# Second pass in chunks of up to 32 tiles spread in three pieces, in place of 24 tiles in two

## The chip, the cores and the metric

The kernel runs on one NeuronCore of a Trainium2 chip. The metric is device time in microseconds (us) of one launch; lower is better. Engines are named as the profile names them: PE (TensorE, the matmuls), PEld (its weight loads), DVE (VectorE), ACT (ScalarE), POOL (GpSimd), SP (the queue that issues most plain DMAs).

## What is computed

A graph layer over N = 10,000 nodes and E = 640,000 edges, all in float32. Each edge takes the row of its source node (64 channels by 4 components, 1 KB), multiplies it by an edge weight and a small coupling tensor, and adds the result into its destination node.

```python
R = silu(edge_feat @ w_rad)                      # (E, 64)
xs = x[src]                                      # (E, 64, 4)
tp = einsum('eci,ef,ifo->eco', xs, Y, cg)        # (E, 64, 4)
msg = R[:, :, None] * tp
agg = segment_sum(msg.reshape(-1, 256), dst, N).reshape(N, 64, 4)
return einsum('ncm,cd->ndm', agg, w_mix)
```

## The kernel before

**Sorting edges by destination.** A sum over edges can only be a matmul when the edges of one tile share a small range of destinations. So the edges are sorted twice. An edge travels as 9 float32 numbers (`W = 9`: a packed key of source and destination, 4 of `Y`, 4 of `edge_feat`), 36 bytes. The first pass (`pass1`) reads edges in tiles of 128 and routes them into 20 groups of nodes in DRAM (`grp`). The second pass (`pass2`) reads one group and routes it into 16 buckets of up to 32 nodes each (`bkt`). The edges come in three parts of 30, 35.5 and 34.5 %, so that the message stage of one part runs while later parts are still being sorted.

**One routing step** (`route`, both passes). A chunk is a run of up to `T` tiles, here 24 in both passes. Per chunk:

- `places` (PE, lines 585 and 586) and `placed` (DVE, 596) and `slots` (DVE, 605 to 607) turn counts into a row and a slot for every edge.
- The chunk is handled in pieces; before, two halves. Per piece, `spread` (DVE, 617 and 623) writes each edge's 9 numbers into its slot of a wide row `X`, and `onehots` writes a 128 by 128 matrix `oh` for each tile that says which row an edge goes to. Of a piece's tiles ACT makes the last `self.act` (6 in the second stage of the program; lines 639 and 640), DVE the others (635).
- `move` (PE, 650) does one matmul per tile, `oh` as weights and `X` as the moving operand, into one PSUM bank `pr` of the chunk. A tile can only fall into slots `lo[t]` to `hi[t]`, so its matmul is `9 * (hi[t] - lo[t])` columns wide: 36 for the first tile of a chunk, 144 for the 24th of the second pass.
- `evict` (ACT, 660, and 662 for the rest of the row) copies the bank to SBUF as `rt`, and `store` (POOL, 669) writes it with one indirect DMA: 128 rows of `S` slots of 36 bytes, S = 35 in the second pass.

The step of a piece is `k`; `evict`, `move`, `places` and the rest run at fixed distances from it (`lag`, `ls` and the constants 5 to 8 in `route`).

**Messages** (`messages`). A unit is one bucket's tiles of one part, 5 or 6 tiles. POOL gathers the source rows, one indirect DMA per tile (944); PE turns and multiplies the edge features (987, 999); ACT applies silu (1003); DVE multiplies (1014, 1021); PE sums 12 matmuls per unit (1032); the sum goes to `Gp` or `Gs` (1061, 1063); at the end `mix` (1080) applies `w_mix`. Gathers run 5 units ahead, into 7 buffers `xg`.

**What sets the order.** In the second stage PE, DVE and ACT keep the order in which the code emits the work; `groups` emits the messages' quarter steps and, between them, as many steps of pass 1 of the next part and of pass 2 of the next group as each needs to be done in time (`pass2_steps` counts them). POOL and SP take their DMAs in a row each. Tables of a group (`tables`) are made once for one or two groups, with one row per chunk.

**After the last unit**, `overflow` handles edges that found no place, 640 at a time, in a loop whose count is read on the chip.

The lines on which the change bears most:

```python
def pieces(self, m):

    return [(0, (m + 1) // 2), ((m + 1) // 2, m)]
...
self.p2 = Pass(T, MB, P // MB, rates, 1.5, 5e-9)
...
v = max(m - self.act, 0)
```

## Time and profile before

| | |
|---|---|
| time, median of 3 runs | 8055.66 us (8052.32 to 8060.37) |
| span of the profiled execution | 9825.7 us |
| mean granted PE clock in it | 0.826 |
| busy share of its span: PE, DVE, ACT, POOL | 74 %, 66 %, 40 %, 59 % |
| indirect DMAs on POOL: gathers, stores of pass 1, stores of pass 2 | 5321, 240, 260 |

The profiled execution is longer than the timed runs; the page has no other time of it than its span. The program has three stages in that span: pass 1 of the first part alone (to 570 us), the mixed stage (pass 1 of the other parts until about 6300 us, pass 2 until about 9450 us, messages until 9740 us), and the overflow at the end. A row of a group of instructions reads: line, engine, operation, out<-in, shapes, count | busy us, mean ns of one | idle us of the engine ahead of them, and what ended it. "issue" is idle time that the profile explains by nothing; "remote" is a wait whose releaser it can't name. On POOL the time between the starts of two DMAs says more than the busy share, as DMA-issuing time is partly not counted. One matmul in float32 leaves two records of MATMUL, so x24 are 12 matmuls.

### The profile page before, as it was taken

The numbers are of one execution on the slowest core, as the hardware profiler recorded it, in microseconds if no ns is written. First come the engines' busy times: TensorE is split into PE (matmuls) and PEld (weight loads), VectorE is DVE, ScalarE is ACT, GpSimd is POOL, SyncE is SP. The second block draws the span as 40 slices with busy tenths as digits, with TensorE's granted clock in tenths as the row PEclk, the third lists the DMA queues.
The fourth block names the chain that finished last, engine by engine and source line by source line (L and its number), as shares of the span: only waits on it lengthen the run. The fifth ranks groups of instructions, "written<-read, shape, count | busy, mean of one in ns | idle before, by whom it ended". The sixth has DMA issues, their size and how long they took to land. (4 is left out here: it accounts for less than half of the span.)

```text
span 9825.7 us, 140823 instructions
## 1 busy us (share of the span) xinstructions
PE 7295.1 (74%) x49703; PEld 6709.1 (68%) x49703; DVE 6455.1 (66%) x10943; ACT 3911.8 (40%) x10964; POOL 5796.5 (59%) x6162
## 2 busy tenths in 40 slices
PE   7968877777776777777777777666776777776765
PEld 6867777777776776766767776666676666666664
DVE  8966777767765766777777776565555565555543
ACT  5754544445543443433434344232232332332321
POOL 4645555555556655555565655666666666666664
PEclk8978888888888888888888888787787888878787
DMA  4323333333333334444444443444433434334332
GB/s 185 109 71 105 105 102 101 99 105 102 107 97 113 109 103 116 114 118 116 115 116 113 123 115 111 127 120 121 113 111 111 115 109 115 111 109 111 103 111 67
DMA packets 680536, 1086.77 MB, mean 111 GB/s; under 512 B 255617, under 2 KB 485099, under 8 KB 673552
## 3 DMA queue, kind: packets, MB, share of 16 engines
q0 software_dynamic: 282224, 774.70, 27.8%
q1 hardware_dynamic: 397600, 303.00, 10.4%
q8 instruction: 395, 6.47, 0.3%
q14 instruction: 317, 2.60, 0.1%
HBM read 855.30 MB, written 222.83 MB: 110 GB/s over the span
## 5 line engine op out<-in xcount | busy, mean ns | idle before, releaser
L944 POOL DMA_INDIRECT xg<-in_x_dram,sidx x5321 | 5067.0, 952 | 3304.7 <-issue 1405.5
L1032 PE MATMUL G<-S,xg 128*128 128x128 f32 x21284 | 3317.3, 320 | 961.2 <-issue 391.9
L1032 PEld LDWEIGHTS G<-S,xg 128*128 128x128 f32 x21284 | 3099.7, 231 | 1070.4 <-issue 481.2
L650 PE MATMUL pr<-X,oh 128*128 128x117 f32 (+15 forms) x20530 | 3037.3, 306 | 694.6 <-issue 424.8
L650 PEld LDWEIGHTS pr<-X,oh 128*128 128x128 f32 x20530 | 2837.2, 214 | 858.9 <-issue 515.0
L1021 DVE TENSOR_TENSOR xg<-xg,pre 128x1536 f32<-128x1536 f32 (+1 forms) x939 | 1556.7, 1658 | 293.2 <-ACT pre L1003 158.9
L639 ACT ACTIVATE oh<-i,row 128x128 f32<-128x128 f32 x5322 | 1653.7, 391 | 81.7 <-remote 29.1
L1003 ACT ACTIVATE pre<-pre 128x384 f32<-128x384 f32 (+1 forms) x939 | 429.9, 458 | 3137.0 <-remote 1191.7
L623 DVE TENSOR_TENSOR X<-dv,Wt 128x1512 f32<-128x1512 f32 (+12 forms) x814 | 1337.0, 1642 | 345.2 <-remote 149.6
L1014 DVE TENSOR_TENSOR S<-dv,pay 128x768 f32<-128x768 f32 (+1 forms) x939 | 857.6, 913 | 140.1 <-remote 70.4
L640 ACT ACTIVATE oh<-oh,ones 128x768 f32<-128x768 f32 (+1 forms) x1000 | 862.8, 863 | 32.2
L1061 DVE TENSOR_TENSOR Gs<-old,G 128x256 f32<-128x256 f32 x313 | 131.6, 421 | 1063.2 <-remote 635.9
L635 DVE TENSOR_TENSOR oh<-dv,row 128x768 f32<-128x768 f32 (+3 forms) x960 | 796.0, 834 | 0.1
L991 ACT ACTIVATE sT<-pre 108x256 bf16<-108x256 bf16 x939 | 353.8, 377 | 800.0 <-remote 475.4
L596 DVE TENSOR_REDUCE pos<-pp 128x24 f32<-128x480 f32 (+9 forms) x500 | 267.4, 535 | 528.5 <-remote 333.3
L987 PE MATMUL pre<-idb,E 128*108 128x128 bf16 x1878 | 297.2, 243 | 341.9 <-DVE xg L1021 130.2
L987 PEld LDWEIGHTS <-E 128*108 128x108 bf16 x1878 | 234.1, 145 | 417.9 <-issue 213.4
L999 PE MATMUL pre<-wr,sT 108*128 108x192 bf16 x1878 | 334.3, 261 | 223.1 <-ACT sT L991 137.7
L669 POOL DMA_INDIRECT bkt<-rt,idx x260 | 259.5, 998 | 312.7 <-ACT rt L662 146.8
L1061 DVE TENSOR_TENSOR Gp<-old,G 128x256 f32<-128x256 f32 x313 | 130.8, 418 | 476.8 <-remote 324.5
L999 PEld LDWEIGHTS <-sT 108*128 108x128 bf16 x1878 | 185.6, 108 | 306.8 <-ACT sT L991 155.3
L669 POOL DMA_INDIRECT grp<-rt,idx x240 | 276.7, 1153 | 174.0 <-issue 51.3
(304 smaller groups left out, 4598.7 us busy)
## 6 DMA issues: line engine op xcount, KB each, us to landing
xg<-in_x_dram,sidx POOLq DMA_INDIRECT x5321
sums<-Gp SPq DMA_DIRECT2D x626, 128.0 KB
old<-sums SPq DMA_DIRECT2D x626, 128.0 KB
bkt<-z SPq DMA_DIRECT2D x26, 1024.0 KB
grp<-z SPq DMA_DIRECT2D x23, 1024.0 KB
pay<-bkt SPq DMA_DIRECT2D x208, 54.0 KB
out_dram<-ot SPq DMA_DIRECT2D x69, 128.0 KB
ys<-in_Y_dram SPq DMA_DIRECT2D x65, 96.0 KB
```

Source lines behind the costliest of these rows:

```text
L623: eng.tensor_tensor(X[:, b:e], msk[:, b:e].unsqueeze(3).to_broadcast([P, e - b, w, W]), CH[c][1][:, a + b:a + e, :].unsqueeze(2).to_broadc ...
L635: nc.vector.tensor_tensor(oh[:, :v, :], self.v128.unsqueeze(1).to_broadcast([P, v, P]), row[:, a:a + v].unsqueeze(2).to_broadcast([P, v, P ...
L639: nc.scalar.activation(oh[:, u], self.i128[:, :oh.shape[2]], AF.Square, bias=row[:, a + u:a + u + 1], scale=-1.0)
L640: nc.scalar.activation(oh[:, v:m], oh[:, v:m], AF.Relu, bias=self.ones[:, 0:1], scale=-2.0)
L650: nc.tensor.matmul(PR[c][:, ps.lo[t] * W:ps.hi[t] * W], oh[:, u, :], Xs[u], start=(t == 0), stop=(t == sizes[c] - 1), skip_group_check=True)
L669: nc.gpsimd.indirect_dma_start(out=ps.dst, out_offset=bass.IndirectOffsetOnAxis(ap=idx[:Q, i:i + 1], axis=0), in_=RT.pop(c), in_offset=None)
L944: nc.gpsimd.indirect_dma_start(out=xg[:, t, :], out_offset=None, in_=self.x, in_offset=bass.IndirectOffsetOnAxis(ap=si[:, u:u + 1], axis=0))
L987: nc.tensor.transpose(to[:108, h * P:(h + 1) * P], E[:, o + h * 108:o + h * 108 + 108], self.idb)
L999: nc.tensor.matmul(R[:, h * 192:h * 192 + n * 64], sT[:n * 36, h * P:(h + 1) * P], self.wr[:n * 36, :n * 64], start=True, stop=True)
L1014: nc.vector.tensor_tensor(S[:, :ut], self.eq[:, :ut].unsqueeze(3).to_broadcast([P, ut, NB, 4]), pb[:, :, 1:5].unsqueeze(2).to_broadcast([P ...
L1021: nc.vector.tensor_tensor(V, V, R.unsqueeze(3).to_broadcast([P, ut, 64, 4]), op=OP.mult)
L1032: nc.tensor.matmul(G[:, h].rearrange("p n f -> p (n f)"), V[:, t, 32 * h:32 * h + 32, :].rearrange("p c i -> p (c i)"), S[:, t].rearrange( ...
```

## The change

`Pass` gets a number of pieces, `cuts`: 2 for the two kinds of pass 1, as before, and 3 for the second pass, whose `T` goes from 24 to 32. A piece has at most `H = ceil(T / cuts)` tiles, so 11 in place of 12, and `pieces` cuts a chunk evenly into as few pieces as fit. Pass 1's chunks come out as before.

With these numbers and the same tiles (5265 in pass 2), the code's own planning gives:

| second pass | before | after |
|---|---|---|
| chunks, each with one store | 260 (160 in the first two parts, 100 in the last) | 200 (120 and 80) |
| pieces | 520 (480 of 9 to 12 tiles, 40 of 3) | 560 (540 of 8 to 11 tiles, 20 of 6) |
| slots S, bytes of a stored row | 35, 1260 | 45, 1620 |
| matmul columns, mean per tile; largest | 100; 144 | 112.8; 171 |
| tiles wider than 144 columns | 0 | 645 (450 in the first two parts) |
| numbers written into `X`, per partition | 638,766 | 687,339 |
| `oh` made by DVE, by ACT (tiles) | 2265, 3000 | 1905, 3360 |

`route` finds the steps of a chunk by its first piece (`first`) in place of by even and odd `k`; the distances in pieces stay. `rt` of pass 2 has 2 buffers in place of 3. `oh` is 12 tiles in both passes.

```diff
-    def __init__(self, T, B, R, rates, low, miss):
-        self.T, self.B, self.R, self.Q, self.H = T, B, R, B * R, (T + 1) // 2
+    def __init__(self, T, B, R, rates, low, miss, cuts=2):
+        self.T, self.B, self.R, self.Q, self.cuts, self.H = T, B, R, B * R, cuts, -(-T // cuts)
...
     def pieces(self, m):
 
-        return [(0, (m + 1) // 2), ((m + 1) // 2, m)]
+        at = [0] + list(itertools.accumulate(even(m, self.H)))
+        return list(zip(at, at[1:]))
...
-        N, E, T = self.N, self.E, 24
+        N, E, T, T2 = self.N, self.E, 24, 32
...
-        self.p2 = Pass(T, MB, P // MB, rates, 1.5, 5e-9)
+        self.p2 = Pass(T2, MB, P // MB, rates, 1.5, 5e-9, cuts=3)
...
+        self.H = max(late.H, self.p2.H)
...
+        first = {k: c for k, (c, a, _) in enumerate(pieces) if a == 0}
...
-            oh = self.ph.tile([P, ps.H, P], F, name="oh", bufs=3)
+            oh = self.ph.tile([P, self.H, P], F, name="oh", bufs=3)
...
-            rt = RT[c] = self.ph.tile([P, ps.S * W], F, name="rt", tag="rt" + ps.key, bufs=self.rt_bufs)[:Q, :n]
+            rt = RT[c] = self.ph.tile([P, ps.S * W], F, name="rt", tag="rt" + ps.key, bufs=2 if ps.cuts > 2 else self.rt_bufs)[:Q, :n]
...
-            if k % 2 and 0 <= k + 7 < NP:
+            if k + 7 in first:
...
-                places((k + 7) // 2)
-            if k % 2 == 0 and 0 <= k + 6 < NP:
-                placed((k + 6) // 2)
+                places(first[k + 7])
+            if k + 6 in first:
+                placed(first[k + 6])
...
-            if k % 2 and 0 <= k + 5 < NP:
-                slots((k + 5) // 2)
+            if k + 5 in first:
+                slots(first[k + 5])
...
-        n = 2 * len(self.sizes2(k, g))
+        n = sum(len(self.p2.pieces(m)) for m in self.sizes2(k, g))
```

Where instructions stand differently, at two places. First POOL, in the last part, over the stores of one group; `xg` are gathers (x6: six, one unit), `bkt` the stores of pass 2. Before:

```order
L669 DMA bkt_64<-rt_59179,idx_57043 1951488x9
L944 DMA xg_59314<-in_x_dram,sidx_58377 128x256 x6
L944 DMA xg_59400<-in_x_dram,sidx_58377 128x256 x6
L669 DMA bkt_64<-rt_59282,idx_57043 1951488x9
L944 DMA xg_59471<-in_x_dram,sidx_58377 128x256 x6
L669 DMA bkt_64<-rt_59372,idx_57043 1951488x9
L944 DMA xg_59534<-in_x_dram,sidx_58377 128x256 x6
L669 DMA bkt_64<-rt_59510,idx_57043 1951488x9
L944 DMA xg_59574<-in_x_dram,sidx_59390 128x256 x6
L944 DMA xg_59610<-in_x_dram,sidx_59390 128x256 x6
L669 DMA bkt_64<-rt_59572,idx_57043 1951488x9
```

And now:

```order
L672 DMA bkt_64<-rt_60122,idx_58984 1964288x9
L947 DMA xg_60301<-in_x_dram,sidx_59370 128x256 x6
L947 DMA xg_60371<-in_x_dram,sidx_59370 128x256 x6
L672 DMA bkt_64<-rt_60274,idx_58984 1964288x9
L947 DMA xg_60443<-in_x_dram,sidx_59370 128x256 x6
L947 DMA xg_60490<-in_x_dram,sidx_60291 128x256 x6
L672 DMA bkt_64<-rt_60469,idx_58984 1964288x9
L947 DMA xg_60526<-in_x_dram,sidx_60291 128x256 x6
L672 DMA bkt_64<-rt_60488,idx_58984 1964288x9
```

A group of the last part has four stores where it had five, and one or two units of gathers stand between two of them; the row of gathers itself is the same.

Second PE, in the last part, over the `move` matmuls of one chunk: `pr` is the chunk's bank, the second number of the shape the width. Before, a whole chunk of 21 tiles in its two pieces:

```order
L650 MATMUL pr<-X,oh 128x36
L650 MATMUL pr<-X,oh 128x54 x2
L650 MATMUL pr<-X,oh 128x72
L650 MATMUL pr<-X,oh 128x81 x3
L650 MATMUL pr<-X,oh 128x90 x2
L650 MATMUL pr<-X,oh 128x99
L650 MATMUL pr<-X,oh 128x108 x3
L650 MATMUL pr<-X,oh 128x117 x3
L650 MATMUL pr<-X,oh 128x135 x4
L650 MATMUL pr<-X,oh 128x144 x2
```

And now, the third piece of a chunk, behind a unit's sum (`G`), and the first piece of the next chunk:

```order
L1035 MATMUL G<-S,xg 128x128 x12
L653 MATMUL pr<-X,oh 128x144 x5
L653 MATMUL pr<-X,oh 128x162 x4
L653 MATMUL pr<-X,oh 128x36
L653 MATMUL pr<-X,oh 128x54 x2
L653 MATMUL pr<-X,oh 128x72
L653 MATMUL pr<-X,oh 128x81 x3
L653 MATMUL pr<-X,oh 128x90 x2
L653 MATMUL pr<-X,oh 128x99
```

The bank of a chunk is now filled by a third run of wider matmuls before the narrow ones of the next chunk begin.

## Rows read from the trace of the kernel before

**Rows 1.** The page's first block: busy us (share of the span), instructions.
```profile
PE 7295.1 (74%) x49703; PEld 6709.1 (68%) x49703; DVE 6455.1 (66%) x10943; ACT 3911.8 (40%) x10964; POOL 5796.5 (59%) x6162
```

**Rows 2.** Busy time by stage: stretch, length, engines (instructions), PE clock, DMA, GB/s.
```profile
0.00:570.00 570.00, 478.29 (x3426) 420.09 (x3427) 506.71 (x1257) 374.81 (x1161) 302.03 (x416) 0.89 0.37 132
570.00:800.00 230.00, 163.82 (x1090) 147.09 (x1090) 152.84 (x314) 111.96 (x318) 113.33 (x117) 0.78 0.32 89
800.00:6300.00 5500.00, 4199.30 (x29102) 3876.92 (x29102) 3876.03 (x6207) 2432.67 (x6784) 3200.78 (x3337) 0.84 0.39 110
6300.00:9450.00 3150.00, 2251.92 (x14880) 2084.32 (x14880) 1774.21 (x2881) 946.29 (x2572) 1993.17 (x2097) 0.81 0.40 113
9450.00:9700.00 250.00, 149.45 (x907) 136.70 (x907) 97.42 (x132) 33.20 (x89) 162.90 (x173) 0.78 0.39 111
9700.00:9826.00 126.00, 52.38 (x305) 44.03 (x305) 47.85 (x154) 12.90 (x42) 24.27 (x26) 0.69 0.10 27
```

**Rows 3.** Timeline of PE from 7599 us: start, us, instruction, [idle before].
```profile
7601.19 0.23 PE L650 MATMUL pr<-X,oh 128*128 128x81 f32 x1 [1.89 <-issue]
7602.59 0.29 PE L650 MATMUL pr<-X,oh 128*128 128x81 f32 x1 [1.17 <-issue]
```

**Rows 4.** Timeline of POOL from 7604 us.
```profile
7604.40 0.94 POOL L944 DMA_INDIRECT xg<-in_x_dram,sidx  x1 [2.67 <-remote]
7605.65 0.95 POOL L944 DMA_INDIRECT xg<-in_x_dram,sidx  x1 [0.30 <-issue]
...
7620.71 1.00 POOL L669 DMA_INDIRECT bkt<-rt,idx  x1 [0.30 <-issue]
```

**Rows 5.** Groups by line on POOL, 800 to 6300 us.
```profile
L944 POOL DMA_INDIRECT xg<-in_x_dram,sidx x3051 | 2911.5, 954 | 2106.0 <-issue 797.0 <-PE G L1032 622.3 <-remote 250.4
L669 POOL DMA_INDIRECT grp<-rt,idx x145 | 148.9, 1027 | 75.9 <-issue 39.5 <-ACT rt L660 21.0 <-DVE X L623 7.7
L669 POOL DMA_INDIRECT bkt<-rt,idx x141 | 140.9, 999 | 117.6 <-issue 35.1 <-ACT rt L660 25.0 <-ACT rt L662 18.5
```

**Rows 6.** Groups by line on POOL, 6300 to 9450 us.
```profile
L944 POOL DMA_INDIRECT xg<-in_x_dram,sidx x1991 | 1888.8, 949 | 1030.9 <-issue 529.5 <-remote 288.9 <-PE G L1032 99.9
L669 POOL DMA_INDIRECT bkt<-rt,idx x106 | 105.9, 999 | 126.2 <-ACT rt L662 70.1 <-issue 23.0 <-DVE X L623 14.9
```

**Rows 7.** Timeline of PE, pieces of `move`, from stretches at 900, 1000 and 6300 us.
```profile
959.78 2.84 PE L650 MATMUL pr<-X,oh 128*128 128x45 f32 x24
...
1079.15 3.33 PE L650 MATMUL pr<-X,oh 128*128 128x126 f32 x24
...
6301.23 2.71 PE L650 MATMUL pr<-X,oh 128*128 128x108 f32 x22
```

**Rows 8.** Waits of PE, 800 to 6300 us: us in total, times, longest.
```profile
PE pr L650 <- ACT rt L660: 77.4, 47, 4.8
PE pre L987 <- ACT E L977: 61.7, 19, 8.2
PE G L1032 <- ACT Gp L1063: 43.0, 20, 5.1
PE pre L999 <- ACT sT L991: 28.7, 19, 3.3
```

**Rows 9.** Groups by line and form on DVE, the whole span.
```profile
L635 DVE TENSOR_TENSOR oh<-dv,row 128x768 f32<-128x768 f32 x393 | 371.2, 948 | 0.0
L635 DVE TENSOR_TENSOR oh<-dv,row 128x640 f32<-128x640 f32 x354 | 287.3, 812 | 0.0
L623 DVE TENSOR_TENSOR X<-dv,Wt 128x1584 f32<-128x1584 f32 x67 | 121.1, 1808 | 23.1 <-remote 8.6 <-PE pre L987 8.2 <-PE pr L650 2.7
L623 DVE TENSOR_TENSOR X<-dv,Wt 128x1188 f32<-128x1188 f32 x85 | 118.6, 1396 | 8.3 <-remote 2.7 <-PE pr L650 2.5
```

**Rows 10.** Groups by line and form on ACT, the whole span.
```profile
L639 ACT ACTIVATE oh<-i,row 128x128 f32<-128x128 f32 x5322 | 1653.7, 391 | 81.7 <-remote 29.1 <-PE pr L650 22.9 <-DVE row L607 13.4
L640 ACT ACTIVATE oh<-oh,ones 128x768 f32<-128x768 f32 x774 | 723.9, 935 | 25.2
L640 ACT ACTIVATE oh<-oh,ones 128x384 f32<-128x384 f32 x226 | 138.9, 615 | 7.1
```

**Rows 11.** Timeline of the overflow, from 9690 us.
```profile
9755.20 2.53 SPq L1241 DMA_DIRECT2D opay<-bkt  x5
```

More of the change, by code (lines that the diff above doesn't have):

```diff
@@ L169, in __init__ @@
         self.xw = max((z - a) * p.width(a, z) * W for p in (late, self.p2)
-                      for m in range(T // 2, T + 1) for a, z in p.pieces(m))
+                      for m in range(p.H, p.T + 1) for a, z in p.pieces(m))
+        self.H = max(late.H, self.p2.H)
         early.NC, late.NC, self.p2.NC = 18, 6, 2 * max(len(self.sizes2(k, g)) for k in range(len(SPLIT)) for g in range(NG))
@@ L684, in route @@
                 self.pos = ps.key
-                places((k + 7) // 2)
-            if k % 2 == 0 and 0 <= k + 6 < NP:
-                placed((k + 6) // 2)
+                places(first[k + 7])
+            if k + 6 in first:
+                placed(first[k + 6])
                 self.pos = None
-            if k % 2 == 0 and 0 <= k + 8 < NP:
-                CH[(k + 8) // 2] = chunk((k + 8) // 2)
+            if k + 8 in first:
+                CH[first[k + 8]] = chunk(first[k + 8])
             if 0 <= k < NP:
```

## Prediction

> **What bounds the kernel now.** I read the busy shares first [rows 1]: no engine is over 74 % of the span, and POOL, with 59 %, looks idle. Both impressions mislead here, for two reasons.
>
> The first is that the profiled execution is not the timed one: its span of 9825.7 us is 1770 us over the median of 8055.66. The timeline of PE shows where such time can lie: single matmuls of 0.2 to 0.3 us with more than a microsecond of "issue" between them [rows 3], while POOL has a gap of 2.67 us put down to "remote" [rows 4]. I take such holes to belong to the profiled execution, and set the engines' own work against the timed 8056 us instead.
>
> The second is that busy time doesn't count all that POOL does. Between the end of one indirect DMA and the start of the next lie 0.30 us for which nothing waited: 0.95 busy, 1.25 from start to start, and the same ahead of a store [rows 4]. POOL's work is then 5796.5 busy [rows 1] plus 0.30 x (5321 gathers + 500 stores) = 7543 us. POOL is not busy for 268 us of the first 570 and 102 of the last 126 [rows 2]. Of the 8056 us this leaves 8056 - 7543 - 370 = 143 us in which POOL does nothing in the 8056 - 696 = 7360 us of the mixed stage: it is 98 % occupied, if the cadence holds outside the profile. PE's busy time in the same stage is 164 + 4199 + 2252 + 149 = 6764 us [rows 2], 92 %; DVE's 5900, 80 %; ACT's 3524, 48 %.
>
> By stage: from 6300 to 9450 us (no pass 1) POOL needs 1993 + 0.30 x 2097 = 2622 us, PE 2252, DVE 1774 [rows 2]. POOL bounds this stage; its gathers wait for PE's sums for only 99.9 us, and most of the rest of its idle time is the 0.30 and the holes [rows 6]. From 800 to 6300 us POOL needs 3201 + 0.30 x 3337 = 4202 us and PE 4199: they are level, and POOL's gathers wait 622.3 us for PE to free their buffers [rows 5]. What POOL saves here, PE may not give back.
>
> **The change part by part.**
>
> POOL's stores. Pass 2 has 200 chunks in place of 260, so 60 stores fewer, 20 of them in the last part. One costs 0.999 + 0.30 = 1.30 us of POOL [rows 5, 6]. In the last part POOL is the bound: 20 x 1.30 = 26 us off the path. In the first two parts it is 40 x 1.30 = 52 us, of which I take half, 26, with nothing and 52 as the ends: two engines that are level and share buffers.
>
> A stored row grows from 1260 to 1620 bytes; no such DMA is in the trace. The nearest rows are a gather of 1024-byte rows at 954 ns and the store of 1260-byte rows at 999, both of 128 rows [rows 5]: 0.19 ns a byte, so 0.07 us more for each of 200, 14 us. The store of pass 1, 120 rows of 1404 bytes, takes 1027 and agrees. At the other end the difference is one of gather and store and not of bytes: 0. I take the middle, 7.
>
> PE. The routing matmuls become wider, 100 to 112.8 columns on average. A piece of 12 from width 45 on (94 columns on average) takes 2.84 us, one of 11 from 108 on (127) 2.71, one of 12 from 126 on (151, eight of them over 144) 3.33 [rows 7]: 0.237, 0.246 and 0.278 each. Up to 144 columns width is nearly free; the last piece pays 12 x 0.032 = 0.38 us for its eight wide ones, 0.048 each. After the change 645 tiles are over 144: 31 us, of which 22 in the first two parts, where PE counts. The Trainium skill, in "TensorE: Matmul & The Clock Gate", section "Step-by-step: what each phase is for", says that back-to-back throughput is purely the number of columns; by that rule all 12.8 % would be paid, which is worked out below as a rival; the pieces in the trace say that it holds only above some width.
>
> Against this stand 60 chunk boundaries fewer. In the mixed stage each pass has in effect one of the two `pr` banks, and PE waits for ACT to empty it: 77.4 us from 800 to 6300 [rows 8] over 286 chunks [rows 5], 0.27 each, so 11 us for 40. Fewer, longer position and count matmuls may save as much again. I put PE at 0 (between -15 and +22).
>
> DVE. `X`: 48,573 numbers more at (1808 - 1396) / 396 = 1.04 ns [rows 9] are 51 us, and 40 instructions more at the 0.16 left at zero length 6. `oh`: 360 tiles fewer at (948 - 812) = 0.136 us [rows 9] save 49, 60 more instructions at 0.13 cost 8. Masks cost a ninth of `X`'s numbers and 40 starts, about 11; 60 position reductions fewer save about 10. Sum: +17 us on 5900, with 1460 us of the mixed stage in which DVE is free: 0.
>
> ACT. Each piece leaves it six tiles: 360 squares more at 1653.7 / 5322 = 0.311 us are 112 us, 80 six-tile passes more at 0.935 less 40 three-tile ones at 0.615 are 50 [rows 10]; 60 evictions fewer, longer ones, give back about 18. Sum: +144 us on 3912, two thirds of it, 96, in the first two parts. ACT has room, but its row is in order, and PE waits for it: 211 us in four kinds of wait [rows 8] on 2433 us of ACT's work [rows 2], 0.087 per us. 96 x 0.087 = 8 us on the path; the ends are 0 and 96.
>
> Nothing else: pass 1's pieces are the same; two `rt` buffers serve a store that goes out two pieces after its eviction and whose buffer is wanted three or more pieces later; one more megabyte is cleared in pass 1. The overflow runs one round at the end [rows 11]. From the destinations in the inputs and the code's rules I get six late chunks of a bucket over its limit, 576 rows, before and after: one round of 640 either way.
>
> **The sum:** -26 - 26 + 7 + 0 + 0 + 8 = -37 us. Against the profiled span it is 0.4 %; the durations are those of instructions and not of the holes, so I take the same 37 us off the median: **8019 us**, 0.5 % faster.
>
> **Rivals.**
>
> *POOL's whole saving arrives.* If the waits for PE in the first two parts come of the holes (PE and its weight loads are nearly four fifths of the instructions in rows 1 and may suffer most), POOL is the bound throughout: -78 + 7 = -71 us, 7985 us; with the waits that stores themselves cause (ACT's eviction not ready, 43.5 us over 141 stores in rows 5, 0.3 us x 60) 7967. For it: 98 % occupancy. Against: 622.3 us of waits for PE.
>
> *The early saving stays hidden.* PE binds the first two parts: -26 + 7 + 8 = -11, 8045 us, which no measurement of this kernel can tell from no change (about 0.2 %, 16 us).
>
> *ACT takes the path, and the kernel gets slower.* A piece's 2.8 us of ACT (six squares and one pass) stands 80 times more ahead of a unit's transposes and silu in the row. From 20 % of the 96 us on, with no early gain, it eats the 26 + 7 = -19 us; at half it gives 8056 - 19 + 48 = 8085 us, whole 8133. For it: DVE's products and PE's sums of a unit both follow ACT. Against: only 211 us of PE's waits are ACT's.
>
> *PE pays for every column.* Then 12.8 % of 5265 x 0.245 = 1290 us, 165 us, are added, 66 % of the tiles being in the first two parts: 109 - 19 = +90, 8146 us. This is the rule that I set beside rows 7. The step from 94 to 127 columns, 35 % more for 4 % of time, speaks against it.
>
> *The rows don't fit as planned*: a seventh overflowing chunk makes 672 rows and a second round. The round lasts from 9755 us [rows 11] to the last 20 us of the span, about 50: 8019 + 50 = 8069 us.
>
> **How the numbers follow.** The forecast, with its early half between a quarter and three quarters (8005 to 8033), 0.42; whole saving 0.18; hidden 0.19; ACT 0.16; columns 0.03; second round 0.02. Faster by over 0.2 %: 0.42 + 0.18 = 0.60. Within: 0.19 and the ACT rival's mildest part, 0.20. Slower: 0.20. The range goes from 7960, the whole saving with the stores' waits and a little more, to 8085, ACT at half; it leaves out half of the ACT rival, the columns and 0.05 below.
>
> **What would show it.** POOL: 200 stores, each within 0.1 us of 999 ns; in the stretch without pass 1, gathers still 1.25 us apart with few waits for PE, and that stage about 26 us shorter. Before that: POOL's waits for PE per gather (622.3 us over 3051) no larger if the forecast is right, larger by tens of us if the saving is hidden. PE: third pieces at about 0.26 us a matmul, total routing time up by some 30 us; 0.30 or more would mean that columns are paid. ACT busy up by about 144 us with PE's waits on it up by about 8; up by 50 would be the slow rival. A store far over 1.1 us, or DVE instead of POOL ahead of PE's waits, would be things that I have not seen.

## The result: 0.43 % slower, and the profile after

The changed kernel takes 8088.47 us (median of 5 runs, 8086.96 to 8093.91) against 8055.66 us (5 runs, 8051.45 to 8062.69): ratio 1.0043, 95 % interval 1.0032 to 1.0055, 33 us slower. The prediction was 8019 us, 37 us faster, with a range from 7960 to 8085.

The profile of the changed kernel has a span of 8085.2 us, the one of before 9825.7. They can't be set side by side, and why is the first thing that the experiments settle. The kernel before, unchanged, was profiled twice more. One profile has a span of 9967.9 us, and that very execution was timed at 9969.68; the other has 8055.5 and 8057.28. So the program runs at one of two paces, the median of before belongs to the quick one, and, by its span and its granted clock of 0.826 (0.823 and 0.900 in the other two), the profile of rows 1 to 11 to the slow one. The holes in [rows 3] are part of the slow pace, not of profiling. Everything below that says "the kernel before" without more means its profile of 8055.5 us.

The pages' first blocks (busy us, share of the span, instructions), which answer [rows 1]; the kernel before, then the changed one:

```profile
PE 6557.0 (81%) x49703; PEld 6147.7 (76%) x49703; DVE 6419.3 (80%) x10943; ACT 3913.5 (49%) x10964; POOL 5814.6 (72%) x6162
```

```profile
PE 6556.7 (81%) x49490; PEld 6136.7 (76%) x49523; DVE 6453.3 (80%) x10940; ACT 4060.3 (50%) x11257; POOL 5754.6 (71%) x6118
```

PE does the same work, DVE 34 us more, ACT 147 more, POOL 60 less. DVE's 34 us look like the 33 us that were lost, but they don't lie where the time was lost: below, DVE is busy 12 us more in the part that grows by 52 us, and 25 more in the part that grows by 10. One has to see where in the program the time is lost. The gathers are a good clock for that: both kernels issue the same 5321 in the same order, 1565 for the first part, 1878 each for the second and the last. Busy time of each engine from the first gather of a part to the first of the next (in the last part, to its last gather); columns: stretch, length, PE, PEld, DVE, ACT, POOL (instructions), PE clock, DMA share, GB/s. They answer [rows 2]. Before:

```profile
593.04:2903.61 2310.57, 1976.39 (x15591) 1870.76 (x15590) 2038.56 (x3482) 1410.61 (x4025) 1662.43 (x1726) 0.92 0.45 130
2903.61:5481.46 2577.85, 2149.41 (x16701) 2033.89 (x16700) 2243.01 (x3474) 1261.63 (x3429) 1948.03 (x2030) 0.91 0.51 148
5481.46:7955.92 2474.46, 1915.61 (x13742) 1794.88 (x13742) 1591.74 (x2579) 844.09 (x2282) 1874.89 (x1968) 0.88 0.46 132
```

And changed:

```profile
595.10:2957.83 2362.73, 1986.32 (x15505) 1868.98 (x15507) 2050.19 (x3502) 1461.77 (x4124) 1643.80 (x1706) 0.92 0.45 127
2957.83:5546.07 2588.24, 2159.72 (x16629) 2039.30 (x16660) 2267.91 (x3506) 1314.38 (x3546) 1929.73 (x2009) 0.92 0.52 147
5546.07:7995.26 2449.19, 1894.38 (x13681) 1779.83 (x13681) 1587.10 (x2525) 884.33 (x2354) 1855.15 (x1950) 0.86 0.47 133
```

The first part becomes 52 us longer, the second 10; the last becomes 25 shorter. With 2 us at the start and 10 less behind the last gather that is the 30 us between the two spans.

With the 0.30 us ahead of each of its instructions, POOL is occupied before for 1662.4 + 0.30 x 1726 = 2180 of 2311 us in the first part (94 %), 2557 of 2578 in the second (99 %), 2465 of 2474 in the last (99.6 %). So the last part is POOL's, the second all but POOL's, and the first is not. PE is level with POOL in none of them: it is busy for 86, 83 and 77 % of the three parts. In the changed kernel the shares are 91, 98 and again 99.6 %: POOL idles 207 us in the first part where it idled 130.

The groups by line on POOL inside the last part (5700 to 7700 us; busy, mean ns, idle before and releasers), which answer [rows 6]: before, then changed.

```profile
L944 POOL DMA_INDIRECT xg<-in_x_dram,sidx x1509 | 1435.0, 951 | 459.7 <-issue 419.5 <-DMA xg<-in_x_dram,sidx 6.7 <-DMA bkt<-rt,idx 5.5
L669 POOL DMA_INDIRECT bkt<-rt,idx x81 | 81.1, 1001 | 24.7 <-issue 22.8 <-ACT sT L991 0.9 <-ACT pre L1003 0.6
```

```profile
L947 POOL DMA_INDIRECT xg<-in_x_dram,sidx x1529 | 1453.0, 950 | 465.8 <-issue 425.9 <-DMA xg<-in_x_dram,sidx 7.3 <-DVE dv L620 4.9
L672 POOL DMA_INDIRECT bkt<-rt,idx x64 | 63.5, 992 | 19.5 <-issue 15.2 <-ACT E L980 3.0 <-ACT pre L1006 0.6
```

Each row's idle time is about its count times 0.30, so POOL works without a gap; in the same 2000 us it issues 17 stores fewer and 20 gathers more. That is the saving, as it was meant.

### The profile page after: what moved, and what is told of

Read it like the earlier page. It is cut to its first block, busy times and chain, and to the rows that moved or that the text cites. A ratio compares the mean times of both kernels' runs of the same rounds, so it can differ in the third digit from the quotient of the medians.

```text
span 8085.2 us, 140623 instructions
## 1 busy us (share of the span) xinstructions
PE 6556.7 (81%) x49490; PEld 6136.7 (76%) x49523; DVE 6453.3 (80%) x10940; ACT 4060.3 (50%) x11257; POOL 5754.6 (71%) x6118
## 5 line engine op out<-in xcount | busy, mean ns | idle before, releaser
L653 PE MATMUL pr<-X,oh 128*128 128x81 f32 (+15 forms) x20530 | 2756.8, 293 | 352.0 <-DVE oh L638 240.9
L1035 PE MATMUL G<-S,xg 128*128 128x128 f32 x21284 | 2939.0, 301 | 28.7 <-DVE Gp L1064 7.1
L653 PEld LDWEIGHTS pr<-X,oh 128*128 128x128 f32 x20530 | 2615.2, 200 | 457.3 <-DVE oh L638 269.2
L1035 PEld LDWEIGHTS G<-S,xg 128*128 128x128 f32 x21284 | 2789.4, 214 | 72.9 <-DVE Gp L1064 34.7
L642 ACT ACTIVATE oh<-i,row 128x128 f32<-128x128 f32 x5682 | 1762.3, 390 | 34.5 <-PE pr L653 14.4
L638 DVE TENSOR_TENSOR oh<-dv,row 128x640 f32<-128x640 f32 (+4 forms) x1020 | 755.9, 746 | 0.2 <-PE pr L653 0.2
L663 ACT ACTIVATE rt<-pr 120x351 f32<-120x351 f32 (+8 forms) x440 | 189.9, 434 | 668.1 <-DMA bkt<-rt,idx 531.7
L1014 DVE TENSOR_TENSOR dv<-dv,dlc 128x192 f32<-128x192 f32 (+1 forms) x939 | 328.9, 350 | 12.0
L599 DVE TENSOR_REDUCE pos<-pp 128x24 f32<-128x480 f32 (+8 forms) x440 | 257.0, 584 | 61.1 <-PE pp L589 50.3
L1083 PE MATMUL po<-wf,Gs 128*128 128x256 f32 (+1 forms) x1280 | 297.4, 386 | 5.3 <-DVE kov L566 2.5
```

Of the source, the lines that this page charges most:

```text
L638: nc.vector.tensor_tensor(oh[:, :v, :], self.v128.unsqueeze(1).to_broadcast([P, v, P]), row[:, a:a + v].unsqueeze(2).to_broadcast([P, v, P ...
L642: nc.scalar.activation(oh[:, u], self.i128[:, :oh.shape[2]], AF.Square, bias=row[:, a + u:a + u + 1], scale=-1.0)
L653: nc.tensor.matmul(PR[c][:, ps.lo[t] * W:ps.hi[t] * W], oh[:, u, :], Xs[u], start=(t == 0), stop=(t == sizes[c] - 1), skip_group_check=True)
L1035: nc.tensor.matmul(G[:, h].rearrange("p n f -> p (n f)"), V[:, t, 32 * h:32 * h + 32, :].rearrange("p c i -> p (c i)"), S[:, t].rearrange( ...
```

## The experiments

Each kernel was timed beside the kernel before on the same chip. This table has those at the quick pace, with the lengths of the three parts between gathers as above, in us:

| kernel | first part | second | last | median | ratio, 95 % interval |
|---|---|---|---|---|---|
| before | 2310.6 | 2577.8 | 2474.5 | 8055.66 | |
| changed | 2362.7 | 2588.2 | 2449.2 | 8088.47 | 1.0043 [1.0032, 1.0055] |
| changed, three `rt` buffers (a_rt3f) | 2367.8 | 2591.0 | 2448.2 | 8090.71 | 1.0046 [1.0032, 1.0060] |
| changed, ACT makes 7 of a piece's tiles (a_act7) | 2396.7 | 2573.7 | 2449.2 | 8112.61 | 1.0072 [1.0058, 1.0085] |
| before, two `rt` buffers (b_rt2f) | 2324.9 | 2573.1 | 2470.7 | 8070.05 | 1.0020 [1.0011, 1.0029] |
| 32 in the last part alone (h_last32) | 2317.7 | 2574.0 | 2449.0 | 8023.09 | 0.9967 [0.9954, 0.9979] |
| 32 in the first two parts alone (h_first32) | 2371.0 | 2592.2 | 2498.1 | 8158.55 | 1.0137 [1.0121, 1.0152] |
| changed, ACT makes 5 (a_act5) | 2362.1 | 2595.9 | 2448.2 | 8092.28 | 1.0052 [1.0038, 1.0065] |
| 32 in the last part, ACT makes 5 (h_last32_act5) | 2311.2 | 2577.6 | 2449.6 | 8030.43 | 0.9976 [0.9967, 0.9985] |
| before, wider matmuls (b_wide) | 2319.7 | 2580.8 | 2474.6 | 8075.31 | 1.0032 [1.0021, 1.0042] |
| before, first part in chunks of up to 18 (b_p0t18) | 2400.9 | 2577.7 | 2477.7 | 8139.30 | 1.0111 [1.0096, 1.0127] |
| changed, one piece more between one-hots and matmuls (a_lag2) | 2541.9 | 2758.9 | 2470.6 | 8467.48 | 1.0518 [1.0504, 1.0533] |
| 32 in the last part, the same (h_last32_lag2) | 2535.1 | 2804.6 | 2475.3 | 8508.82 | 1.0568 [1.0553, 1.0582] |

A part's length is from one profile. Three kernels with the first part of before (the first row, b_rt2f, h_last32) lie 14 us apart there; less than that is not read from a single row. Of the second part this can be said: in the six kernels of this table (without the two of longer distance) that have the old chunks there it took 2573 to 2581 us, in four of the five with the new chunks 2588 to 2596, and in a_act7 2574. The parts given in the expectations were read a few gathers off; they are up to 9 us from those here, with differences between kernels that are 4 us from these or less.

### The pace

No edit; the kernel before, looked at again.

> The kernel before, unchanged, for a profile without the holes that its first profile had (span 9825.7 us against 8055.66 timed; the profile of the changed kernel has a span of 8085.2). Expected: a span near 8056 us. By my prediction POOL has some 140 us of idle time in the mixed stage, and ACT's evictions wait for no store. If POOL is idle for 150 us or more before the last part, the changed kernel's 219 us there are little worse and the loss lies elsewhere.

> The kernel before again, for a profile at the pace of its timed runs (8056 us); the chip of the first call ran everything at 9900 us and more. Expected at that pace: POOL without gaps in the last part, DVE busy for about 89 % of the first two parts, no evictions that wait for stores. If DVE is below 85 % there while the changed kernel is at 89 %, the changed kernel's DVE work is what grew; if POOL's gathers reach the first gather of the last part about as late as in the changed kernel (5434 us), the loss lies behind it.

The routing matmuls and the gathers from 800 to 5000 us (busy, mean ns, idle before and releasers), at the slow pace:

```profile
L650 PE MATMUL pr<-X,oh 128*128 128x126 f32 (+13 forms) x9933 | 1474.1, 307 | 362.0 <-issue 238.3 <-ACT rt L660 67.2 <-DVE oh L635 36.5
L944 POOL DMA_INDIRECT xg<-in_x_dram,sidx x2275 | 2174.5, 956 | 1676.7 <-issue 588.5 <-PE G L1032 525.8 <-remote 187.6
```

and at the quick one:

```profile
L650 PE MATMUL pr<-X,oh 128*128 128x108 f32 (+12 forms) x12820 | 1684.0, 291 | 170.6 <-DVE oh L635 102.2 <-ACT rt L660 67.2 <-ACT pre L1003 0.8
L944 POOL DMA_INDIRECT xg<-in_x_dram,sidx x2955 | 2826.2, 956 | 991.5 <-issue 787.3 <-PE G L1032 84.4 <-DMA xg<-in_x_dram,sidx 19.5
```

The slow pace has 238 us in which PE stands before routing matmuls and nothing is waited for; the quick one has none worth a row. The gathers' waits for PE are 525.8 us there and 84.4 here, over more gathers. Rows 5 and 8, on which the prediction built the balance of the first two parts, are rows of the former.

The holes are not all of it. The first block of the slow profile, to be set beside the 6557.0 us of PE at the quick pace:

```profile
PE 7341.3 (74%) x49703; PEld 6735.4 (68%) x49703; DVE 6450.1 (65%) x10943; ACT 3910.4 (39%) x10964; POOL 5796.7 (58%) x6162
```

PE's same 49,703 records are busy 784 us longer there, while DVE, ACT and POOL are within 31 us of the quick profile. So [rows 1] and [rows 2] overstate PE's work, and of the four only PE's, for a run of 8056 us.

### The changed kernel at the slow pace, and the rt buffers

The changed kernel with some tiles that are used only at the start or the end moved or held once, which frees room in SBUF (a_trim2), and the same with three `rt` buffers (a_rt3, and a_rt3f at the quick pace). The edit of the first in part, and that of the second on top of it:

```diff
-            di = ph.tile([P, MB, MT], I32, name="didx", bufs=2)
+            di = ph.tile([P, MB, MT], I32, name="didx", bufs=1)
...
-            rt = ... bufs=2 if ps.cuts > 2 else self.rt_bufs)[:Q, :n]
+            rt = ... bufs=self.rt_bufs)[:Q, :n]
```

> The changed kernel with 1.4 KB per partition of other tiles saved (two scratch tiles with one buffer in place of two, two constants of the overflow made at the end) and still two buffers rt in pass 2: the control for a third one. Both theories: as the changed kernel, 8080 to 8095 us.

> The same with three buffers rt in pass 2. Theory 1 (ACT's evictions wait 532 us for the stores of two chunks back, and through ACT's row this makes the kernel slower): those waits vanish and the time falls by 30 to 70 us, to 8015 to 8055. Theory 2 (POOL runs without a gap in the last part, where 494 us of these waits are, so they cost nothing; the loss is made in the first two parts by the wider and more numerous pieces): the waits vanish and the time stays within 16 us of a_trim2, 8070 to 8095.

> The changed kernel with 1.4 KB of other tiles saved and three rt buffers in pass 2, on another chip. Theory 1 (waits of evictions for stores): at the 8056 us pace 30 us or more faster than the changed kernel's 1.0043, so a ratio of 1.000 or less. Theory 2 (DVE in the first two parts): ratio 1.003 to 1.005, as the changed kernel. At the 9900 us pace both give 0.996 to 0.998, as on the first chip.

At the slow pace a_trim2 takes 9898.98 us and a_rt3 9906.56 against 9933.37: ratios 0.9968 (0.9952 to 0.9983) and 0.9967 (0.9952 to 0.9981), 27 to 34 us *faster*. There the first part grows less (2923 us before, 2942 and 2925 in these), the second becomes 44 and 32 us shorter and the last 36 and 31. These lengths are rough: the profile of before that they are set against was timed 36 us over the median of its session, and the profile of rows 1 to 11, of the same kernel, has parts of 2905, 3254 and 2954 us in place of 2923, 3324 and 3009. At the quick pace the same kernel as a_rt3 is 0.46 % slower. One program, two signs.

The third buffer changes nothing at either pace. The wait that it removes is real (ACT's evictions; idle before and releasers over the whole span, changed and a_rt3f):

```profile
L663 ACT ACTIVATE rt<-pr 120x351 f32<-120x351 f32 (+8 forms) x440 | 189.9, 434 | 668.1 <-DMA bkt<-rt,idx 531.7 <-PE pr L653 133.5
```

```profile
L656 ACT ACTIVATE rt<-pr 120x351 f32<-120x351 f32 (+8 forms) x440 | 190.0, 434 | 316.7 <-DMA bkt<-rt,idx 169.3 <-PE pr L646 140.2 <-DMA xg<-in_x_dram,sidx 4.3
```

but 442 of the 532 us lie in the last part, where POOL works without a gap. So buffers are not where the 52 us went.

The other side, two buffers in the kernel before:

```diff
-            rt = ... bufs=self.rt_bufs)[:Q, :n]
+            rt = ... bufs=2 if ps is self.p2 else self.rt_bufs)[:Q, :n]
```

> The kernel before with two buffers rt in pass 2 in place of three, nothing else. Theory 1: slower by 20 us or more (the third eviction waits for a store two pieces behind the first). Theory 2: within 16 us of the kernel before, 8040 to 8072, though waits of evictions for stores appear.

> The kernel before with two rt buffers in pass 2. Theory 1: at the 8056 us pace slower by 20 us or more, ratio 1.0025 or more. Theory 2: within 0.2 % of the kernel before.

1.0003 (0.9988 to 1.0017) at the slow pace; 15 us, 1.0020 (1.0011 to 1.0029), at the quick one. Two buffers are dearer with the old chunks, which take one every two pieces, than with the new, which take one every three.

### ACT's share of a piece

`onehots` gives the last `self.act` = 6 tiles of a piece to ACT, the others to DVE. In pass 2 alone, 7, and later 5:

```diff
-            v = max(m - self.act, 0)
+            v = max(m - self.act - 1 * (ps is self.p2), 0)
```

> The changed kernel, but in pass 2 ACT makes seven tiles of each piece's oh and DVE the others (was six): some 540 tiles move, 73 us less DVE and about 240 us more ACT. Theory 2 (DVE bounds the first two parts, busy for 89 % of them): two thirds of the 73 us come back, ratio 0.997 to 1.000 at the 8056 us pace. The rival that I put on record (ACT's row is what binds): slower still, 1.010 or more. Theory 1: as the changed kernel or a little more, 1.004 to 1.007.

> The changed kernel, but ACT makes five tiles of the one-hots of a piece of pass 2 in place of six, DVE one more: about 220 us less on ACT and 73 us more on DVE. If ACT's row is what the first two parts lose time by (the opposite step, seven tiles, cost 24 us), some 20 us less than the changed kernel, about 8068 us, with the gathers of the first part earlier. If DVE is (89 % busy there), some 20 to 50 us more, 8110 to 8140 us.

Seven costs 24 us more than the changed kernel: the first part loses 34 and the second gives 15 back. Taken alone this would have proved the rival on ACT. Five is the counter-test. The first part of a_act5:

```profile
592.73:2954.84 2362.11, 1992.75 (x15505) 1877.17 (x15507) 2076.11 (x3502) 1389.30 (x3935) 1642.08 (x1706) 0.92 0.45 127
```

Neither of the expected times came: 8092.28 us is the changed kernel's time. ACT is busy 1389 us there, less than in the kernel before (1411), DVE 2076 against 2050 with six, and the part is as long as with six. So ACT's extra work isn't what the change loses by, unless DVE's 26 us more took back what ACT's 72 less gave; in b_wide, below, as much more on DVE goes with 9 us, so there is little to hide behind it. Six stands at the foot of a slope that begins at seven.

### Which part loses, which gains

On a_rt3, chunks of up to 32 in three pieces in the last part alone, with the old ones before it:

```diff
-        at = [0] + list(itertools.accumulate(even(m, self.H)))
+        at = [0] + list(itertools.accumulate(even(m, 12 if m <= 24 else self.H)))
...
-        n, T, end = self.gt[k][g], self.p2.T, 6 if k == len(SPLIT) - 1 else 0
+        n, T, end = self.gt[k][g], 32 if k == len(SPLIT) - 1 else 24, 6 if k == len(SPLIT) - 1 else 0
...
-        p.full = p.last = self.lists(p, c, k + "f", jr, [p.S] * p.NC)
+        p.full = p.last = self.lists(p, c, k + "f", jr, [p.hi[23] if p is self.p2 else p.S] * p.NC)
```

> Chunks of up to 32 tiles in three pieces only in the last part; the first two parts have the chunks of up to 24 in two pieces and three rt buffers, as before. Theory 3 (the last part is POOL's and the 20 stores saved there arrive; what the change loses, it loses in the first two parts): the last gather of the second part issues where it did before (5476 us, where the changed kernel has 5538), the last part is about 23 us shorter than before, and the time is about 8055 - 25 = 8030 us. If the loss has its seat in something that all three parts share (more pieces in ACT's row everywhere), the time stays near 8055 or above it.

8023.09 us, 27 us less than before, ratio 0.9967 (0.9954 to 0.9979). The last part has its 25 us, the first two have their old lengths to within 7 us. This is the fastest of all kernels tried, and it beats both. By the code's planning the last part is also the only one in which the change takes chunks away (20) without adding pieces: 200 before and after, where each of the first two parts goes from 160 to 180.

The complement, 32 in the first two parts (24 and 32 changed places in the edit above; two `rt` buffers):

> The complement: chunks of up to 32 in three pieces in the first two parts, chunks of up to 24 in two pieces in the last; two rt buffers as in the changed kernel. Theory 3: the first two parts lose what the changed kernel loses there (62 us at the last gather of the second part) and nothing is gained in the last: 8055 + 55 to 65, about 8115 us, slower than the changed kernel. If the early loss were no loss of the early parts' own, about 8080 us.

The first two parts lose 60 and 14 us, a little more than in the changed kernel; but the time is 8158.55 and not 8115, because the last part, whose chunks are the old ones, is 24 us longer than before. There POOL has real gaps. One of its waits, and one each of ACT and PE, from 5760 to 7760 us (total, times, longest):

```profile
POOL bkt L665 <- DVE dv L1007: 11.7, 5, 2.4
```

```profile
ACT rt L656 <- DMA bkt<-rt,idx: 584.7, 48, 23.0
```

```profile
PE pr L646 <- ACT oh L636: 163.1, 27, 19.0
```

Two buffers and chunks of two pieces alone don't do this: b_rt2f has both, and its last part is no longer than before. What h_first32 has beside is that the six tiles at the end of a group are one piece in place of two. My reading: with all three together an eviction waits up to 23 us for a store, ACT's row stands behind it, PE waits for one-hots, and in the end POOL's stores come late. So the wait that costs the changed kernel nothing is not harmless in itself: there it stops just short of POOL.

> As the kernel with chunks of up to 32 in the last part alone, but ACT makes five tiles of a piece's one-hots in place of six. It asks whether ACT's row sets the pace of the first part with the old chunks too. If it does: 20 us less than the same kernel with six, about 8010 us. If with the old chunks ACT and DVE were in balance at six: the same or some 10 us more, 8030 to 8045 us.

8030.43 us: with five tiles on ACT the last-part kernel is no faster (0.9976, 0.9967 to 0.9985, against 0.9967, 0.9954 to 0.9979). With the old chunks too the first part doesn't hang on this split.

### Width, pieces, distance

What is left is the shape of the new chunks. The kernel before with lower windows in pass 2, which widens its matmuls to 112.9 columns on average, as in the changed kernel, and its products beyond those of the changed kernel:

```diff
-        self.p2 = Pass(T, MB, P // MB, rates, 1.5, 5e-9)
+        self.p2 = Pass(T, MB, P // MB, rates, 3.0, 5e-9)
```

> The kernel before, its chunks and pieces unchanged, but the windows of pass 2 begin lower, so that the routing matmuls have 112.9 columns on average in place of 100 (the changed kernel: 112.8) and X 725,000 numbers in place of 640,000 (the changed kernel: 687,000). If width is what the first part loses 48 us by (2306 us from its first to its last gather before, 2354 after), that part is 40 to 60 us longer here and the time 8095 to 8120 us. If it is the number of pieces, the part stays within 10 us and the time is 8055 to 8070 us.

The first part grows by 9 us, not 52, the second by 3; the whole by 23 us, 5 us over what was expected for this case, with 98 us more on DVE (the change brings 34). In the first part its mean width is that of the changed kernel (109.6 and 109.5 columns by the planning), and over all parts it has twice as many tiles wider than 144 columns, 1305 against 645. Routing matmuls, before and b_wide, whole span:

```profile
L650 PE MATMUL pr<-X,oh 128*128 128x117 f32 (+15 forms) x20530 | 2687.6, 290 | 276.1 <-DVE oh L635 166.3
```

```profile
L650 PE MATMUL pr<-X,oh 128*128 128x90 f32 (+15 forms) x20530 | 2723.8, 291 | 270.1 <-DVE oh L635 180.7
```

13 % more columns in pass 2 go with 36 us more of PE, which is no more than kernels of equal widths differ by (b_rt2f, with the widths of before, has 2727.5). Width is a small part.

The kernel before with more and narrower pieces in the first part alone: 100 chunks of 15 to 17 tiles and 200 pieces, where there were 80 and 160 (the changed kernel: 60 and 180):

```diff
-        n, T, end = self.gt[k][g], self.p2.T, 6 if k == len(SPLIT) - 1 else 0
+        n, T, end = self.gt[k][g], (18, 24, 24)[k], 6 if k == len(SPLIT) - 1 else 0
```

> The kernel before with chunks of up to 18 tiles in the first part alone: 200 pieces there in place of 160 (the changed kernel: 180), 100 chunks in place of 80, and narrower matmuls (88 columns on average in place of 97). If the pieces cost the first part its time (48 us for 20 more, 2.4 us each), that part becomes 80 to 100 us longer, 8135 to 8155 us. If widths do, it grows by no more than its 20 more stores, 26 us, and the narrower matmuls and products give some back: 8040 to 8080 us.

The first part grows by 90 us, at narrower matmuls, and the time by 87: 1.0111 (1.0096 to 1.0127). Forty pieces more cost 90 us, twenty cost 52. With p a piece and c a chunk, 20p - 20c = 52 and 40p + 20c = 90, so p = 2.4 us and c = -0.2: read like this, the 26 us of POOL that 20 more or fewer stores make are not seen in the length. Two lengths give two prices, so nothing in them checks the reading; 14 us of scatter in a length are 0.2 us in p and some 0.7 in c. The first part of b_p0t18:

```profile
594.53:2995.47 2400.94, 2032.14 (x15627) 1929.07 (x15626) 2008.87 (x3661) 1515.76 (x4322) 1680.09 (x1745) 0.89 0.44 126
```

DVE is busy 30 us *less* than before in a part that is 90 us longer, PE 56 and ACT 105 more. In the changed kernel work explains still less of 52 us: PE 10, DVE 12, and ACT's 51 came off again in a_act5 without effect. So the loss goes with the number of pieces, and most of it isn't work. I read it as the price of their hand-overs; that is a reading of the waits, no experiment has isolated one. What a piece waits for in the first part (595 to 2890 us; total, times, longest), before:

```profile
PE pr L650 <- ACT rt L660: 52.3, 36, 4.7
PE pr L650 <- DVE oh L635: 41.5, 35, 3.0
```

```profile
POOL xg L944 <- PE G L1032: 94.0, 42, 6.6
```

changed:

```profile
PE pr L653 <- DVE oh L638: 66.1, 56, 3.5
PE pr L653 <- ACT rt L663: 50.8, 30, 5.0
```

```profile
POOL xg L947 <- PE G L1035: 141.1, 57, 9.3
```

and b_p0t18:

```profile
PE pr L650 <- ACT rt L660: 73.8, 41, 4.2
PE pr L650 <- DVE oh L635: 38.1, 31, 3.6
PE pr L650 <- ACT oh L640: 37.2, 27, 10.3
```

```profile
POOL xg L944 <- PE G L1032: 162.1, 64, 8.9
```

PE waits more often at a piece's start, for one-hots in the changed kernel, for ACT's share of them and the bank in the other; the sums behind come later, and POOL's gathers wait for those: 47 and 68 us more, most of what the part grew by. The measure is rough: in a_act5 that wait is 159.3 us, 18 more than in the changed kernel, in a part of the same length.

One rival for b_p0t18 is left. Its pieces have 7 to 9 tiles of which ACT still makes six, so that ACT is busy 1516 us in the first part: close to the 1535 us of a_act7, where ACT's seventh tile cost 34 us. PE's wait for ACT's one-hots, 0.5 us before and 12.5 in the changed kernel in this stretch, is nearly as long in a_act7 as in b_p0t18:

```profile
PE pr L653 <- ACT oh L643: 33.5, 31, 3.5
```

If 34 of the 90 us were ACT's, a piece would cost 1.9 us and not 2.4. No run has the many pieces with a smaller share for ACT. That the number of pieces is the cause is thus argued, by taking width, buffers and ACT's sixth tile away one by one; it is not shown by itself.

The obvious remedy, more distance between a piece's one-hots and its matmuls:

```diff
-        lag = self.lag
+        lag = self.lag + (ps is self.p2)
```

> The changed kernel, but in pass 2 the routing matmuls of a piece (and its eviction) stand two pieces behind its one-hots in place of one. Cover theory: a piece has fewer tiles and follows sooner on the one before, so PE reaches a piece's matmuls before its one-hots are made (172 us of waits for them from 800 to 5200 us, 105 before). Then PE's waits for oh nearly vanish and 30 to 50 us come back, 8040 to 8060 us. If the wait is only where PE happens to sit while something else sets the pace, it moves to another line and the time stays within 10 us of 8088.

> Chunks of up to 32 in the last part alone, with the same longer distance from one-hots to matmuls. Cover theory: the old chunks of the first two parts wait for their one-hots too (105 us from 800 to 5200), so some 20 to 40 us come off 8023: 7985 to 8005 us. Otherwise 8015 to 8035 us.

Both expectations fail by hundreds of microseconds: 8467.48 and 8508.82, ratios 1.0518 and 1.0568. PE's waits for DVE's one-hots do fall (66.1 to 43.2 us in the first part), and another takes their place (a_lag2, same stretch, waits of DVE):

```profile
DVE X L626 <- PE pr L653: 267.8, 98, 7.4
```

54 us of it in the changed kernel. `X` and `oh` have three buffers. A matmul that comes one piece later gives its buffer back one piece later, to a product that stands in DVE's row ahead of the messages. So I read a piece as held from both sides, by inputs that come late and by buffers that come free late; measured is that with three buffers a distance of two is far worse than one. A fourth buffer was not tried.

### Fewer pieces

Two kernels take pieces away in the first part: the last-part kernel with three chunks of 21 to 23 and one of 12 there (140 pieces), and the changed kernel with chunks of 32, 32 and the rest (153 in place of 180). Both also clear the end of `rt` in steps of 128 columns, which a short last chunk needs.

```diff
-        return even(n - end, T) + [end] * (end > 0)
+        if k == 0:
+            end = 12
+        return even(n - end, T) + [end] * (end > 0)
```

```diff
+        if k == 0:
+            return [T, T, n - 2 * T]
         return even(n - end, T) + [end] * (end > 0)
```

> Chunks of up to 32 tiles in the last part, and in the first part three chunks of 21 to 23 tiles and one of 12 in place of four of 18 to 21: the same 80 chunks and tiles, but 140 pieces in place of 160, each nearly full. If the first part pays by the piece (48 us for 20 more, 92 for 40 more, so 2.3 to 2.4 us each), 46 us come off it and the time is 8023 - 46, about 7977 us. If the earlier losses came of something that went along with the pieces (ACT's squares fall here too, by 120, 47 us; but five tiles in place of six on ACT moved nothing), or if POOL or another engine is next in the first part at once, 8005 to 8025 us.

> The changed kernel, but the 75 to 81 tiles of a group in the first part are cut into chunks of 32, 32 and the rest in place of three equal ones: the same 60 chunks and tiles, matmuls a little wider, 153 pieces in place of 180. By the price of a piece the first part is 60 to 65 us shorter than in the changed kernel, which takes the time to about 8025 us. If width or the size of a chunk is what costs, it is no shorter: 8085 to 8100 us.

10180.04 and 10871.58 us against 9933.07 for before: ratios 1.0250 (1.0229 to 1.0270) and 1.0941 (1.0917 to 1.0964). They decide nothing on pieces at the quick pace, for two reasons that only the traces show. They ran at the slow pace. And a chunk of 11 to 17 tiles at the end of a part sends rows to the overflow. A round there has five gathers; over the whole span a_p0 has 20 rounds, h_last32_p0 5, the kernel before and the changed one have 1. The row of a_p0:

```profile
L1269 POOL DMA_INDIRECT oxg<-in_x_dram,osi x100 | 95.6, 956 | 124.5 <-DVE odst L1264 100.1 <-issue 15.3 <-DVE oeq L1275 4.3
```

From a_p0's last gather at 9784.0 us to its end at 10876.8 lie 1093 us, in the kernel before at that pace 115: 51 us for each of the 19 rounds more. Without them: at the slow pace the first part has 2905 and 2923 us in two profiles of before, 2925 in a_rt3 and 2942 in a_trim2 with 20 pieces more, 2924 in a_p0 with 7 fewer than before, and 2977 in h_last32_p0 with 20 *fewer*. These lengths don't follow the number of pieces: by 2.4 us each, a_p0 would lie 65 us under a_rt3 and a_trim2. What lengthens the part in h_last32_p0 is open. At the quick pace the price is read from kernels with more pieces only; that fewer would give it back is not shown.

## Why the prediction was wrong, point by point

**The rows and the median were of two paces.** I took the holes for a trace of profiling, set the engines' work against 8056 us and took the balance of the first two parts from rows 5 and 8. The forecast of 37 us faster is close to what this change does at the pace of those rows (27 to 34 us, a_trim2 and a_rt3). How far that is more than luck is open, since the parts are known there only to some tens of us. At the pace of the median the sign is another. I assumed that the durations of rows 1 and 2 carry over, and PE's don't: its work, 92 % of the mixed stage by my sum, is 82 % of the three parts at the quick pace (6041 of 7363 us); POOL's 98 % holds (7202 us with the 0.30). The sign that something was off stood in the table of times itself: a span 1770 us over the median. An execution timed and profiled in one would have settled it; lacking that, the range should have been built from both.

**-26 in the last part: right.** 25 us in the changed kernel, 25 in h_last32, with POOL 99.6 % occupied before and after.

**-26 for half of the early stores: the step that failed.** I called POOL (4202 us) and PE (4199) level over the two parts together and split the saving between them. At the quick pace they are not level: in the first two parts POOL is occupied for 4737 us and PE busy for 4126, less than DVE (4282). In the first part POOL is only 94 % occupied, and 20 stores fewer bring nothing: the part becomes 52 us longer. In the second it is 99 %, the 26 us were POOL's to give, and yet the part came out 10 us longer, 36 us over what POOL alone would have made of it. The two together: 62 us longer where I had 26 shorter.

**What was missing: a price of the pieces.** The change makes 40 pieces more in the first two parts, and I priced them by what they add to each engine's busy time: DVE +17 on the whole (34 came), ACT +144 (147 came), PE +0 (the total is the same). DVE's came out at twice the sum, the others as summed, and none of them explains the loss. In the first part 20 pieces more go with 52 us, while PE is busy 10 us more for all of them and DVE 12. Such a price stands nowhere among my terms or rivals. What in a piece costs it stays open.

**The ACT rival** gave 8085 us at half and so comes nearest in number, but its mechanism falls: with ACT back at 1389 us in the first part nothing is regained (a_act5). It is true of the seventh tile.

**PE and width: right in kind, low in size.** Third pieces have nine tiles in 2.49 us, 0.277 each, second pieces ten in 2.43, 0.243 (timeline of PE in the last part; each tile is two matmuls in it):

```profile
6110.58 2.43 PE L653 MATMUL pr<-X,oh 128*128 128x108 f32 x20
6119.69 2.49 PE L653 MATMUL pr<-X,oh 128*128 128x144 f32 x18
```

This is the step up beyond 144 columns that rows 7 had shown. All routing matmuls took 2756.8 us against 2687.6, 69 more where I had said some 30, of which b_rt2f's 40 us at unchanged widths make a part uncertain; PE's total didn't rise. By the rule of the Trainium skill that I had set beside them ("TensorE: Matmul & The Clock Gate", "Step-by-step: what each phase is for") it would have been 165; b_wide, with the same mean width and 36 us, agrees with the rows and not with that rule.

**+7 for longer rows: nothing.** A store of 1620-byte rows took 1003 ns (mean of 200), one of 1260 bytes 1005 (260): of the two bounds it was the zero.

**"Two `rt` buffers serve": right here, not in general.** They cost the changed kernel nothing (a_rt3f), the old chunks 15 us (b_rt2f), and in h_first32, with the old chunks and the six tiles in one piece, the last part is 24 us longer.

**One overflow round: right**, and my price for a second, about 50 us, was measured by accident: 51.

## What to carry to other kernels

A saving on the bounding engine counts only in the stages where that engine is occupied without a gap: cut the trace by a landmark that both kernels share, give each stage its own occupancy, and apply the change there alone; here 0.43 % slower became 0.33 % faster. When work is cut into more pieces, allow for a price of the piece beside that of its work, and measure it with a kernel that changes the number of pieces and nothing else, since a part can grow by 52 us while PE and DVE are busy 10 and 12 us more. And before a row is used, see that the profiled execution ran at the pace of the timed ones.

## What the hardware showed that was not expected

The two paces. In two of the experiments' five sessions (the first and the last) the kernel before took 23 % more than in the others, 9933 against 8050 to 8056 us, with no overlap between runs of one pace and the other; the two experiments that ran at both, b_rt2 and a_rt3, took 23 and 22 % more. The record names the same chip, number 6, for the first session and for the second, which was quick, so the pace doesn't go with that number. The mean granted clock of TensorE over the span was 0.82 there and 0.90 here for the kernel before. What the slow pace adds can be seen on PE, as above: its instructions take 784 us more, and it stands before matmuls with nothing to wait for. Whether the lower clock makes the holes or the holes the lower clock, and what sets the pace, can't be read from these traces.

ACT and DVE can trade one tile in a piece, 72 us of ACT for 26 of DVE in the first part, without a trace in its length, while the next tile the other way costs 34 us there. A balance that is flat on one side and steep on the other can't be found by testing one side.
